# A spectral mixing and snake kernel on one Trainium2 core: batch 0's last stage in groups of 3, 5 and 4 row columns, and batch 2's input loaded behind batch 1's relayout

## The chip, the cores and the metric

The kernel runs on one core of a Trainium2 chip. The metric is the device time of one execution in microseconds (us). The core has a tensor engine for matmuls (TensorE, PE), a vector engine (VectorE, DVE), a scalar engine (ScalarE, ACT), GpSimd (POOL) and SyncE (SP); the last three and ScalarE also issue DMA transfers here. Results of matmuls go to PSUM, and are evacuated to SBUF by VectorE or ScalarE.

## The reference

Two blocks follow each other. The first filters each sequence of x (8 batches, 3008 positions, 256 channels) in the frequency domain; the second is a two-layer network on every position, with a "snake" between its layers.

```python
X = np.fft.rfft(x, axis=1)                       # x: (8, 3008, 256)
Y = X * (filt_r + 1j * filt_i)[None, :, :]
y = np.fft.irfft(Y, n=x.shape[1], axis=1)
# positions of all batches as rows: (24064, 256)
h = y @ w_in                                     # d_ff = 2048
s = np.sin(alpha * h)
out = (h + s * s / (alpha + 1e-09)) @ w_out      # (24064, 256) float32
```

## The kernel before

**The filter.** The sequence of 3008 = 32 × 94 positions is seen as 32 "row columns" (n) of 94 rows. A Fourier transform is done in two stages of small matmuls with tables, and back in two stages. For a batch from 1 on this is the class `Spectral`: `load_x` (line 140, POOL queue) brings x as 4 tiles of 8 row columns, rounded to fp16; `first` (line 180) multiplies with the table wf into PSUM tile pa, which is evacuated and stored to DRAM by the SP queue (d1, line 185); `load_t2` (line 192, POOL queue, 8 transfers a batch) reads it back in another layout: this pair is the relayout. `forward` (line 200, PSUM tile pb) has twelve steps u; ScalarE evacuates each to an fp16 tile xf (line 203), and two DMAs of the SP queue swap its halves into xs (line 207). `product` (line 214) and `cross` (lines 220 and 221) multiply with the filter on VectorE; `inverse` (line 231, PSUM tile pc) follows, stored to DRAM as d2 by the SP queue (line 238) and read back by it (`load_t4`, line 243). `last` (line 258, PSUM tile pd, 4 row columns and half the channels at a time) gives y, in fp16, with the channels on the partitions. The pools have 4 buffers for x, 3 for xf, 3 for xs, and 2 PSUM tiles for all of pa, pb, pc and pd.

**Batch 0** doesn't go through DRAM: code before the main loop does its four stages with transposes on VectorE (line 385) in place of the relayout. Its inverse stage `inverse_0` (line 422) needs the table e_t, which comes in two halves of 384 KB behind the filter's loads (line 315), all on the POOL queue. Its last stage is also in `last` (line 255: two matmuls for each row column, one for each half of the partitions). The first 8 row columns are done before the main loop (lines 488 to 492), for channels 0 to 127 and 128 to 255 in turn; the rest in the main loop, by `last_two`, a pair of groups of 4 row columns, one for each half of the channels. `evac` (lines 156 to 161) does an evacuation on ScalarE (line 159) or VectorE (line 161), by its argument or in a turn of three.

**The network** works on chunks of 512 (or 384) columns of y, that is of positions. A chunk takes 8 steps of the main loop (lines 620 to 631). In `hidden` (lines 507 to 513) two matmuls give a PSUM tile ph of 128 features, from which ScalarE makes a cosine (line 510) and VectorE the snake v (line 511). In `project` (lines 523 to 532) the chunk before is multiplied with w_out into po, copied by ScalarE (line 529) and stored by `store` (line 549), in pieces that the order of rows dictates. The pieces alternate between the SP queue and a second queue: ScalarE's for the last two tiles of the last chunk, POOL's for the other tiles of that chunk, SP again otherwise.

**The order** of all instructions is written by hand. The filter of the later batches runs between the network's matmuls: `put` (line 557) gives each of its operations a due time in steps, and `slot` (line 597) emits at every half step what is due, in that order. So the due times set what stands behind what in each engine's and each queue's order. The due times that matter here are those of x of batch 2 (line 578), of batch 0's later pairs (line 572) and, unchanged, those of batch 1's t2 loads (12.5, line 582) and of its forward steps (from 17.5, line 585).

Of the kernel before, what the change touches and what calls it, by code (L numbers as in the profile page):

```python
# [10 lines left out]
FP32 = mybir.dt.float32  # L11
# [11 lines left out]
NR = 2 * N1  # L23
NK = 4 * NS
# [38 lines left out]
def kernel(  # L63
# [10 lines left out]
    nc = tc.nc  # L74
# [6 lines left out]
    e_dram = nc.inline_tensor(e_host, name="e_tbl")  # L81
# [10 lines left out]
    def pool(name, bufs, space=None):  # L92
        kw = {} if space is None else {"space": space}
        return ctx.enter_context(tc.tile_pool(name=name, bufs=bufs, **kw))
# [11 lines left out]
    fps = pool("fps", 2, PSUM)  # L106
# [5 lines left out]
    t4_h = [cpool.tile([128, 16, C], FP16, name=f"t4_h{i}") for i in range(2)]  # L112
# [6 lines left out]
    y = cpool.tile([128, 2, 2, 32, NR], FP16)  # L119
# [4 lines left out]
    for h in range(2):  # L124
        nc.sync.dma_start(out=x32[:, 4 * C * h:4 * C * h + 4 * C],
                          in_=bass.AP(tensor=x.tensor, offset=x.offset + 4 * h * C, ap=[[32 * C, 96], [1, 4 * C]]))
    nc.scalar.dma_start(out=wf0_t, in_=wf0_dram.ap())
    d_t = cpool.tile([128, NS, 128], FP16)
    e_t = cpool.tile([128, NS, 128], FP16)
    wi_t = cpool.tile([NK, NR], FP16)  # L130
    wi0_t = cpool.tile([128, NR], FP16)
# [24 lines left out]
    def evac(dst, src, on_act=None):  # L156
        flip[0] = (flip[0] + 1) % 3
        if flip[0] if on_act is None else on_act:
            marks["act"] = nc.scalar.copy(out=dst, in_=src)  # L159
        else:  # L160
            marks["dve"] = nc.vector.tensor_copy(out=dst, in_=src)  # L161

    class Spectral:
# [79 lines left out]
            nc.sync.dma_start(out=t4_h[ch // 2][0:NK, r0:r0 + 8, :],  # L243
                               in_=self.d2_rows[:, 8 * ch:8 * ch + 8, :])

        def last(self, u, on_act=None):
            ch, rest = divmod(u, 4)
            half, cb = divmod(rest, 2)
            n0 = 8 * ch + 4 * half
            ps = fps.tile([128, 4, 128], FP32, name=f"pd_{self.b}_{u}", tag="f")  # L250
            psv = ps.rearrange("p a b -> p (a b)")[:, 0:4 * NR].rearrange("p (a r) -> p a r", r=NR)
            for i in range(4):
                if self.b == 0:
                    for k in range(2):
                        nc.tensor.matmul(out=psv[64 * k:64 * k + 64, i, :], lhsT=t4_0[cb][:, n0 + i, :, k],  # L255
                                         rhs=wi0_t, start=True, stop=True)
                else:
                    nc.tensor.matmul(out=psv[:, i, :], rhs=wi_t, start=True, stop=True,  # L258
                                     lhsT=t4_h[ch // 2][0:NK, n0 % 16 + i, cb * 128:cb * 128 + 128])
            evac(y[:, cb, self.b % 2, n0:n0 + 4, :], psv, on_act)  # L260

        def last_two(self, u):
            self.last(u, True)
            self.last(u + 1, False)

    warm = cpool.tile([128, 1], FP32)
    nc.vector.memset(warm, 0.0)
# [18 lines left out]
    def split_alpha():  # L286

        nc.gpsimd.tensor_copy(out=one[0:16], in_=id32)
        for i, part in enumerate(parts):
            src = rest if i else al  # L290
            nc.gpsimd.tensor_copy(out=part[0:16], in_=src)
            if i < 2:
                nc.gpsimd.tensor_tensor(out=rest, in0=src, in1=part[0:16], op=ALU.subtract)
# [10 lines left out]
    for g in range(2):  # L304
        gs = slice(12 * g, 12 * g + 12)
        for k, filt in enumerate((filt_r, filt_i)):
            for q in range(2):
                if (g, k, q) == (0, 1, 1):
                    split_alpha()
                off, step = ((12 * g) * C, C) if q == 0 else ((N1 - 12 * g) * C, -C)  # L310
                marks["filt", g, k] = nc.gpsimd.dma_start(
                    out=f_t[k][64 * k + 32 * q:64 * k + 32 * q + 32, gs, :],
                    in_=bass.AP(tensor=filt.tensor, offset=filt.offset + off,
                                ap=[[N1 * C, 32], [step, 12], [1, C]]))
        nc.gpsimd.dma_start(out=e_t[:, gs, :], in_=e_dram.ap()[:, gs])

    idle = opool.tile([128, 512], FP32, name="idle", tag="o")
    nc.vector.memset(idle, 0.0)
# [2 lines left out]
    def pairs(t):  # L321

        return t.rearrange("p a (b s k) -> p s (a b) k", s=32, k=2)
# [5 lines left out]
    t1_0, t2_0, g_0, t4_0 = pairs(t1_0), [pairs(t) for t in t2_0], [pairs(t) for t in t1_h], [pairs(t) for t in t4_h]  # L329
# [38 lines left out]
    for i in range(16):  # L368
        own, tag = (fps, "f") if i % 3 == 2 else (hps, "h")
        ps = own.tile([128, 512], FP32, name=f"pa_0_{i}", tag=tag)  # L370
        nc.tensor.matmul(out=ps, lhsT=wf0_t[0:NR], rhs=x0[i // 4][:, 2 * (i % 4):2 * (i % 4) + 2, :],
                         start=True, stop=True)
# [43 lines left out]
    def inverse_0(i):  # L416
# [7 lines left out]
                                 start=(k == 0), stop=(k == 1))  # L424
        evac(g_0[hc][:, 4 * w:4 * w + 4], ps.rearrange("p s (k c) -> p s c k", k=2), not (i in ()))

    w1 = cpool.tile([128, 2, DFF], FP16)
    w2 = cpool.tile([128, 16, C], FP16)
    after(nc.sync.dma_start(out=wi0_t, in_=wi0_dram.ap()), marks["filt", 0, 1])
# [2 lines left out]
    for g in range(6):  # L432
        own, tag = (t2pool, "t2") if g < 3 else (gpool, "g")
# [17 lines left out]
        if g == 0:  # L451
            after(ins, marks["products"])

    s0 = Spectral(0)

    [inverse_table(g) for g in range(2)]
    for i in range(6):
# [27 lines left out]
    for step in ([(weights_in, g) for g in range(6)] + [(s1.load_x, 0), (s1.load_x, 1)]):  # L485
        step[0](*step[1:])
    warm_pe(2)
    s0.last(0, True)
    s0.last(2, True)
    warm_pe(3)  # L490
    s0.last(1, True)
    s0.last(3, False)

    chunks = [(pb, c0, 384 if c0 == 2560 else 512) for pb in range(B // 2)
              for c0 in [*range(0, 2561, 512), *range(2944, 2 * S, 512)]]
# [19 lines left out]
    def project(k, u):  # L515

        pb, c0, n = chunks[k]
        t, half = divmod(u, 2)
        final = k == len(chunks) - 1 and t > 1
        if (t % 2 == 0 or final) and half == 0:  # L520
            pso[k] = ops.tile([128, 2, C], FP32, name=f"po_{k}_{t}", tag="o")
        for jb in range(8 * half, 8 * half + 8):
            nc.tensor.matmul(out=pso[k][:, t % 2, :], lhsT=v[k][:, jb, 128 * t:128 * t + 128],  # L523
                             rhs=w2[:, jb, :], start=(jb == 0), stop=(jb == 15))
        last = 128 * (t + 1) == n
        if half == 1 and (t % 2 == 1 or last or final):
            i0 = t % 2 if final else 0
            o = opool.tile([128, 2, C], FP32, name=f"o_{k}_{t}", tag="o")
            nc.scalar.copy(out=o[:, i0:t % 2 + 1, :], in_=pso[k][:, i0:t % 2 + 1, :])  # L529
            for i in range(i0, t % 2 + 1):  # L530
                store(o[:, i, :], pb, c0 + 128 * (t - t % 2 + i),
                      nc.scalar if final else nc.gpsimd if k == len(chunks) - 1 else nc.sync)

    def runs(cnt):

        whole = cnt if max(d for d in range(1, 17) if cnt % d == 0) > 7 else cnt - cnt % 16
        return [(0, whole), (whole, cnt - whole)] if 0 < whole < cnt else [(0, cnt)]

    def store(o_blk, pb, col, second):

        p = 0
        queues = [nc.sync, second]
        while p < 128:
            odd, rest = divmod(col + p, S)
            n2, row = divmod(rest, NR)
            cnt = min(128 - p, NR - row)
            t0 = (2 * pb + odd) * S + 32 * row + n2
            for i, (r0, rows) in enumerate(runs(cnt)):
                queues[i].dma_start(  # L549
                    out=bass.AP(tensor=out.tensor, offset=out.offset + (t0 + 32 * r0) * C,  # L550
                                ap=[[32 * C, rows], [1, C]]),
                    in_=o_blk[p + r0:p + r0 + rows, :])
            p += cnt
# [3 lines left out]
    def put(at, fn, *args, pe=False):  # L557
        pending.append((at, len(pending), pe, fn, args))
# [9 lines left out]

    for i in range(2):
        put(13 + i, negate, i)  # L570
    for u in range(4, 16, 2):
        put((1,3,4.5,6,14,16)[u // 2 - 2], s0.last_two, u, pe=True)
    for b in range(1, B):
        s = s1 if b == 1 else Spectral(b)
        z = 48 * b
        if b > 1:
            for ch in range(4):
                put((22,27,32,37)[ch] if b == 2 else z - 92 + 7 * ch, s.load_x, ch)
        for i in range(16):
            put(7.5 + 0.3 * i if b == 1 else 36 + 0.66 * i if b == 2 else z - 67 + 0.66 * i, s.first, i, pe=True)  # L580
        for g in range(4):
            put(12.5 if b == 1 else max(z - 56, 46.5), s.load_t2, g)
        for u in range(12):
            inv = 23.5 + 1.25 * u if b == 1 else 59 + 2.1 * u if b == 2 else z - 40.8 + 2.3 * u
            fwd = inv - (6 if b == 1 else 6)
            put(fwd, s.forward, u, pe=True)
            put(fwd + (0.5 if b == 1 else 1.5), s.product, u)
            if s.fused:
                put(fwd + (4 if b == 1 else 4.5), s.cross, u)
            put(inv, s.inverse, u, pe=True)  # L590
        for ch in range(4):
            put(z - (9.5 if b == 1 and ch < 3 else (10.5, 10.5, 10.5, 3)[ch]), s.load_t4, ch)
        for u in range(16):
            put(z + (u - (5 if b == 1 else 6.5) if u < 4 else 2 * u - 9), s.last, u, pe=True)
# [68 lines left out]
```

## Time and profile before

| what | before |
|---|---|
| time, median of 3 runs | 789.39 us (788.52 to 789.53) |
| span of the profiled execution | 789.0 us |
| TensorE busy | 776.2 us, 98% |
| VectorE busy | 657.4 us, 83% |
| ScalarE busy | 617.0 us, 78% |
| GpSimd busy | 79.7 us, 10% |
| bytes moved by DMA | 101.01 MB, 128 GB/s |
| granted TensorE clock | 1.00 |

In the profile, a line such as "L510 ACT" is an operation of ScalarE written at line 510. "x3" behind an operation is a count. In a timeline, the two leading numbers are the start and the duration in us, and the bracket at the end is the idle time of the engine before the operation, with what ended it. "SPq", "ACTq" and "POOLq" are the DMA issues of an engine. In the views of DMA, q0 holds what POOL issues and q1 what SP and ScalarE issue.

The early part of the run, up to about 62 us, is batch 0's filter and the weights' loads. Batch 1's filter then runs beside the network's first chunks until about 120 us, and each later batch's beside the chunks of the batches before it. The last transfers of the output end the run.

### The profile page before, as it was taken

The page shows a single profiled execution, that of the slowest core. Times are in us where ns is not written, and L with a number is a line of the kernel's source. Part 1 is how long each engine was busy: PE and PEld are TensorE (multiplying, and loading weights), DVE is VectorE, ACT ScalarE, POOL GpSimd, SP SyncE. Part 2 cuts the span into 40 slices and gives each one's busy share as a digit, 9 for nine tenths or more (in the row PEclk, how much of TensorE's full clock was granted, in tenths as well). Part 3 has the DMA queues.
Part 4 walks back from the last instruction along what each step waited for, and adds up shares of the span by engine and source line. Part 5 has one row for each costly group of instructions (what it writes and reads, how often), then busy time and mean ns, then how long its engine had stood idle before and what let it go on. Part 6 is the DMA issues. An engine that isn't in the chain of part 4 may idle for free.

```text
span 789.0 us, 16730 instructions
## 1 busy us (share of the span) xinstructions
PE 776.2 (98%) x5854; PEld 536.3 (68%) x5854; DVE 657.4 (83%) x1171; ACT 617.0 (78%) x1209; POOL 79.7 (10%) x125
## 2 busy tenths in 40 slices
PE   8999989999999999999999999999999999999997
PEld 4756757676667766777666766777666776766666
DVE  7887987899878997799978998799987999777773
ACT  6887868888878887888887888788887887777663
POOL 6442000200020000200020000200002000000000
PEclk9999999999999999999999999999999999999999
DMA  9956568755573646554575455845566233421111
GB/s 217 257 105 173 118 144 206 173 104 134 140 198 82 135 98 191 150 121 102 121 210 124 100 106 137 219 94 113 128 165 171 62 97 82 116 62 29 41 41 54
DMA packets 87677, 101.01 MB, mean 128 GB/s; under 512 B 14472, under 2 KB 75928, under 8 KB 87592
## 3 DMA queue, kind: packets, MB, share of 16 engines
q1 hardware_dynamic: 78016, 73.73, 34.5%
q0 software_dynamic: 9360, 26.15, 17.4%
q8 instruction: 46, 0.75, 0.4%
q14 instruction: 39, 0.32, 0.1%
q10 hardware_dynamic: 216, 0.05, 0.0%
HBM read 55.72 MB, written 46.66 MB: 130 GB/s over the span
## 4 chain that ended last, share of the span: by engine, by line
PE 90%; DVE 2%; DMA 2%; ACT 2%; issue 1%; POOL 1%; SPq 1%; ACTq 0%; POOLq 0%; DVEq 0%
PE po L523 40%; PE ph L507 40%; PE pa L180 3%; PE pd L258 2%; PE pb L200 2%; PE pc L231 2%; DMA e_t<-e_tbl 1%; DVE v L511 1%; PE pd L255 1%; DMA xs<-xf 1%; ACT cos_all L510 1%; DVE t_h L385 1%; SPq L549 1%; ACT t_h L159 1%; DVE t_h L161 0%
## 5 line engine op out<-in xcount | busy, mean ns | idle before, releaser
L511 DVE SCALAR_TENSOR_TENSOR v<-cos_all,ph 128x512 f16<-128x512 f32 (+1 forms) x768 | 482.8, 671 | 107.4 <-ACT cos_all L510 103.9
L510 ACT ACTIVATE cos_all<-ph 128x512 f32<-128x512 f32 (+1 forms) x768 | 410.9, 592 | 99.5 <-PE ph L507 98.3
L523 PE MATMUL po<-w,v 128*128 128x256 f16 x3008 | 388.7, 272 | 0.0
L507 PE MATMUL ph<-y,w 128*128 128x512 f16 (+1 forms) x1536 | 386.4, 374 | 0.5 <-DVE y L161 0.3
L523 PEld LDWEIGHTS <-v 128*128 128x128 f16 x3008 | 289.3, 98 | 78.2 <-issue 1.2
L507 PEld LDWEIGHTS <-w 128*128 128x128 f16 x1536 | 147.5, 98 | 104.5 <-issue 2.5
L529 ACT COPY o<-po 128x512 f32<-128x512 f32 (+1 forms) x97 | 55.6, 573 | 19.6 <-PE po L523 12.6
L203 ACT CAST xf<-pb 128x512 f16<-128x512 f32 x84 | 50.0, 595 | 15.2 <-PE pb L200 13.8
L192 POOL DMA_DIRECT2D t<-d x56 | 36.3, 666 | 202.4 <-DMA out_dram<-o 128.6
L159 ACT CAST t_h<-pa 96x512 f16<-96x512 f32 x74 | 43.3, 586 | 8.5 <-PE pa L180 8.3
L140 POOL DMA_DIRECT2D x<-in_x_dram x32 | 17.1, 535 | 302.1 <-PE pc L231 171.4
L159 ACT CAST y<-pd 128x376 f16<-128x376 f32 x83 | 40.0, 482 | 7.6 <-PE pd L258 5.3
L258 PEld LDWEIGHTS <-t_h 96*128 96x128 f16 x448 | 31.4, 97 | 18.4 <-issue 0.4
L180 PE MATMUL pa<-x,wf_t 94*96 94x512 f16 x112 | 42.2, 381 | 1.0 <-DVE t_h L161 0.6
L159 ACT CAST g<-pc 128x512 f16<-128x512 f32 x58 | 34.4, 593 | 9.4 <-PE pc L231 9.0
L221 DVE TENSOR_TENSOR p<-p,xs 128x512 f16<-128x512 f16 x84 | 35.7, 425 | 2.9
L220 DVE TENSOR_TENSOR xs<-xs,filt_t 128x512 f16<-128x512 f16 x84 | 35.0, 416 | 2.8 <-DMA xs<-xf 2.8
L258 PE MATMUL pd<-wi_t,t_h 96*128 96x94 f16 x448 | 37.1, 204 | 0.0
L214 DVE TENSOR_TENSOR p<-xf,filt_t 128x512 f16<-128x512 f16 x84 | 35.0, 416 | 0.0
L231 PE MATMUL pc<-p,e_t 128*128 128x256 f16 x168 | 32.1, 273 | 1.7 <-DVE p L221 1.7
L200 PE MATMUL pb<-t,d_t 128*128 128x256 f16 x168 | 32.1, 272 | 0.5 <-DVE g L161 0.4
L161 DVE CAST t_h<-pa 96x512 f16<-96x512 f32 x38 | 25.9, 681 | 0.7 <-PE pa L180 0.5
(66 smaller groups left out, 257.5 us busy)
## 6 DMA issues: line engine op xcount, KB each, us to landing
x<-in_x_dram POOLq DMA_DIRECT2D x30, 376.0 KB, 5.0
d<-t_h SPq DMA_DIRECT2D x28, 384.0 KB
t<-d POOLq DMA_DIRECT2D x56, 192.0 KB, 4.6
xs<-xf SPq DMA_DIRECT2D x168, 64.0 KB
d<-g SPq DMA_DIRECT2D x56, 192.0 KB
t_h<-d SPq DMA_DIRECT2D x28, 384.0 KB
out_dram<-o SPq DMA_DIRECT2D x104, 80.0 KB
w_out<-in_moe_w_out_dram SPq DMA_DIRECT2D x1, 2048.0 KB
```

The lines of the kernel that those rows point to most:

```text
L159: marks["act"] = nc.scalar.copy(out=dst, in_=src)
L180: marks["pe"] = nc.tensor.matmul(out=ps[0:NK, :], lhsT=wf_t, rhs=self.x[ch][:, 2 * j:2 * j + 2, :], start=True, stop=True)
L192: nc.gpsimd.dma_start(out=self.t2[g][64 * p:64 * p + 64, :, :], in_=self.d1[a0:a0 + 6, :, :].rearrange("s n c -> n s c"))
L200: nc.tensor.matmul(out=ps[:, i, :], lhsT=d_t[:, s, :], rhs=self.t2[s // 6][:, s % 6, :], start=True, stop=True)
L203: nc.scalar.copy(out=self.xf[u], in_=ps)
L231: nc.tensor.matmul(out=ps[:, i, :], lhsT=e_t[:, 2 * w + i, :], rhs=pt[:, i, :], start=(k == 0), stop=(k == len(pr) - 1))
L258: nc.tensor.matmul(out=psv[:, i, :], rhs=wi_t, start=True, stop=True, lhsT=t4_h[ch // 2][0:NK, n0 % 16 + i, cb * 128:cb * 128 + 128])
L507: nc.tensor.matmul(out=ps[:, 0:n], lhsT=w1[:, cb, jb * 128:jb * 128 + 128], rhs=y_cols[:, cb, c0:c0 + n], start=(cb == 0), stop=(cb == 1))
L510: nc.scalar.activation(out=cs[:, 0:n], in_=ps[:, 0:n], func=AFT.Sin, bias=float(np.pi / 2))
L511: marks["snake"] = nc.vector.scalar_tensor_tensor(out=v[k][:, jb, 0:n], in0=cs[:, 0:n], scalar=-1.0, in1=ps[:, 0:n], op0=ALU.add, op1=ALU. ...
L523: nc.tensor.matmul(out=pso[k][:, t % 2, :], lhsT=v[k][:, jb, 128 * t:128 * t + 128], rhs=w2[:, jb, :], start=(jb == 0), stop=(jb == 15))
L529: nc.scalar.copy(out=o[:, i0:t % 2 + 1, :], in_=pso[k][:, i0:t % 2 + 1, :])
```

## The change

It has four parts. The first four columns of the table e_t get a load of their own, ahead of the imaginary filter. Batch 0's last stage is cut into groups of 3, 3, 5, 5, 4, 4, 4 and 4 row columns in place of eight groups of 4: the first chunk of 512 columns needs row columns 0 to 5 only, which are now all that is done before the main loop. The two evacuations of a later pair are done by one engine, VectorE and ScalarE in turn, where each pair had one on each. The loads of x of batch 2 are due at steps 14 to 18.5 in place of 22 to 37, which puts them on the POOL queue directly behind batch 1's t2 loads, and takes them out of the time in which batch 1's later half-swaps run. And in the last chunk, the second block of a pair of tiles is stored by the POOL queue alone, which leaves SyncE's queue to the first block and to the final tiles.

```diff
@@ filter and table loads
         for k, filt in enumerate((filt_r, filt_i)):
+            if (g, k) == (0, 1):
+                nc.gpsimd.dma_start(out=e_t[:, 0:4, :], in_=e_dram.ap()[:, 0:4])
             for q in range(2):
...
-        nc.gpsimd.dma_start(out=e_t[:, gs, :], in_=e_dram.ap()[:, gs])
+        es = slice(4 if g == 0 else 12, 12 * g + 12)
+        nc.gpsimd.dma_start(out=e_t[:, es, :], in_=e_dram.ap()[:, es])
@@ batch 0's last stage
-    def last_two(self, u):
-        self.last(u, True)
-        self.last(u + 1, False)
+    def last_0(cb, n0, n1, on_act):
+        ps = fps.tile([128, 4, 128], FP32, name=f"pd_0_{cb}_{n0}", tag="f")
+        psv = ps.rearrange("p a b -> p (a b)")[:, 0:(n1 - n0) * NR].rearrange("p (a r) -> p a r", r=NR)
+        for n in range(n0, n1):
+            for k in range(2):
+                nc.tensor.matmul(out=psv[64 * k:64 * k + 64, n - n0, :], lhsT=t4_0[cb][:, n, :, k],
+                                 rhs=wi0_t, start=True, stop=True)
+        evac(y[:, cb, 0, n0:n1, :], psv, on_act)
+
+    def last_two(i, n0, n1):
+        last_0(0, n0, n1, ([i % 2 == 1] * 2)[0])
+        last_0(1, n0, n1, ([i % 2 == 1] * 2)[1])
...
-    s0.last(0, True)
-    s0.last(2, True)
+    last_0(0, 0, 3, True)
+    last_0(0, 3, 6, True)
     warm_pe(3)
-    s0.last(1, True)
-    s0.last(3, False)
+    last_0(1, 0, 3, True)
+    last_0(1, 3, 6, False)
@@ the last chunk's stores
-                      nc.scalar if final else nc.gpsimd if k == len(chunks) - 1 else nc.sync)
+                      *(nc.sync, nc.scalar) if final else (nc.gpsimd if i else nc.sync, nc.gpsimd)
+                      if k == len(chunks) - 1 else (nc.sync, nc.sync))
@@ due times
-    for u in range(4, 16, 2):
-        put((1,3,4.5,6,14,16)[u // 2 - 2], s0.last_two, u, pe=True)
+    for i, n0 in enumerate((6, 11, 16, 20, 24, 28)):
+        put((1,3,4.5,6,14,16)[i], last_two, i, n0, (11, 16, 20, 24, 28, 32)[i], pe=True)
...
-                put((22,27,32,37)[ch] if b == 2 else z - 92 + 7 * ch, s.load_x, ch)
+                put((14,15.5,17,18.5)[ch] if b == 2 else z - 92 + 7 * ch, s.load_x, ch)
```

More of the change, by code (lines that the diff above doesn't have):

```diff
@@ L244, in load_t4, with last @@
                                in_=self.d2_rows[:, 8 * ch:8 * ch + 8, :])
-        def last(self, u, on_act=None):
+        def last(self, u):
             ch, rest = divmod(u, 4)
@@ L252, in last @@
             for i in range(4):
[L253 to L260, printed above, removed]
-        def last_two(self, u):
-            self.last(u, True)
-            self.last(u + 1, False)
+                nc.tensor.matmul(out=psv[:, i, :], rhs=wi_t, start=True, stop=True,
+                                 lhsT=t4_h[ch // 2][0:NK, n0 % 16 + i, cb * 128:cb * 128 + 128])
+            evac(y[:, cb, self.b % 2, n0:n0 + 4, :], psv)
     warm = cpool.tile([128, 1], FP32)
@@ L452, in weights_in @@
             after(ins, marks["products"])
-    s0 = Spectral(0)
     [inverse_table(g) for g in range(2)]
@@ L537, in runs, with store @@
         return [(0, whole), (whole, cnt - whole)] if 0 < whole < cnt else [(0, cnt)]
-    def store(o_blk, pb, col, second):
+    def store(o_blk, pb, col, *queues):
         p = 0
-        queues = [nc.sync, second]
         while p < 128:
```

## The prediction

> **What bounds the kernel now.** I begin with the page: section 1 for the shares, section 4 for the chain that sets the end.
>
> ```profile
> PE 776.2 (98%) x5854; PEld 536.3 (68%) x5854; DVE 657.4 (83%) x1171; ACT 617.0 (78%) x1209; POOL 79.7 (10%) x125
> PE 90%; DVE 2%; DMA 2%; ACT 2%; issue 1%; POOL 1%; SPq 1%; ACTq 0%; POOLq 0%; DVEq 0%
> ```
>
> TensorE is busy for 776.2 of 789.0 us. The change keeps every matmul of the reference's work (batch 0's last stage stays at 128), so it can win only the idle 12.8 us. The second view, TensorE's waits by stretch, says where that idle time is: before 62 us, and between 62 and 140. From 140 to 780 it lists none.
>
> ```profile
> PE pd L255 <- ACT y L159: 0.6, 1, 0.6
> PE pc L422 <- DMA e_t<-e_tbl: 0.5, 1, 0.5
> ...
> PE pc L422 <- DVE p L412: 0.5, 1, 0.5
> ```
>
> These are from 0 to 62 us (total, times, longest). The third view, busy time by stretch (columns PE, PEld, DVE, ACT, POOL, clock, DMA share, GB/s), shows the one hole after that.
>
> ```profile
> 75.00:85.00 10.00, 10.00 (x73) 6.94 (x72) 8.45 (x16) 8.26 (x17) 0.00 (x0) 1.00 0.56 131
> 95.00:110.00 15.00, 14.64 (x107) 10.29 (x106) 14.83 (x32) 11.97 (x25) 1.05 (x2) 1.00 0.71 145
> 110.00:120.00 10.00, 8.11 (x53) 4.81 (x51) 7.11 (x15) 6.46 (x12) 0.00 (x0) 1.00 0.56 137
> ```
>
> In 110 to 120, TensorE lacks 1.89 us and VectorE has time too: neither engine is the limit, something is waited for. The timelines of TensorE and VectorE name it.
>
> ```profile
> 117.03 0.39 PE L231 MATMUL pc<-p,e_t 128*128 128x256 f16 x2 [1.46 <-DVE p L221]
> ```
> ```profile
> 116.09 0.42 DVE L220 TENSOR_TENSOR xs<-xs,filt_t 128x512 f16<-128x512 f16 x1 [2.83 <-DMA xs<-xf]
> ```
>
> The last half-swap (xs of u=11) of batch 1, issued at 109.57 and 110.08, is late by 2.83 us. The DMA shares by queue at 109 to 111 us (packets, MB, share of 16 engines) say why:
>
> ```profile
> q0 software_dynamic: 58, 0.23, 79.7%
> q1 hardware_dynamic: 9, 0.01, 1.5%
> ```
>
> That is the third x load of batch 2 (q0, the POOL queue, issued 107.68): while it runs, the SP queue (q1) gets almost nothing. At 98 to 100 us, behind the load issued at 96.62, it is 98.2% to 1.1%.
>
> [...] under t2 loads (71 to 77 us) q1 still has 17.1% beside q0's 81.9%; under x loads 1.1 to 1.5%. So x loads are bad neighbours for swaps wherever they stand. [...] the last POOL store took 1.86 us (782.73 to 784.59), the last SP store 1.78 (786.15 to 787.93). [...]
>
> **Part A, e_t's first 128 KB ahead of filt_i.** The first pc waits 0.54 us for e_t, at 21.53. But what follows is bound by filt_i of the second half: VectorE's copy at 25.12 waits for that DMA, the products follow, and pc of block 6 starts only at 27.05, after 0.46 us for p. Only the loop of pc and its evacuation behind it (two PSUM slots) can begin 0.4 earlier, up to the turn at 30.38, which waited 0.47 for its last evacuation. I take a gain of 0.2. The edit adds one DMA and no bytes, but puts 128 KB ahead of 12 filter rows; if all of that delay reached the turn it would cost 0.3. Range −0.2 to +0.3.
>
> **Part B, groups of 3, 5 and 4.** Before the main loop, each half takes 12 matmuls where it had 16: 4 × 0.0725 us (16 take 1.16) = 0.29, and its evacuation shrinks from 376 to 282 columns. [...] So the first ph after the wait at 36.79 comes some 0.3 earlier. The pairs of rows 6 to 11 then take 20 matmuls where 16 stood, and give the 0.29 back. The wait at 45.01 (0.56 us) is for the previous evacuation on ScalarE, by the queue's order of the two PSUM slots; with both evacuations of this pair on VectorE it goes. Against it: the next pair, 20 to 24, puts a second 478 ns on ScalarE, which has no idle time between 46.26 and 53.96. Net 0.56 − 0.48 = 0.1. The pairs at steps 14 and 16 meet idle time on either engine (0.35 to 0.5 on VectorE, 1.42 on ScalarE near 69 to 71): 0. Sum for B 0.1, from −0.3 to +1.0, the top if ScalarE catches up elsewhere. A and B: −0.3.
>
> **Part C, x of batch 2 at steps 14 to 18.5.** The loads leave 85.11, 96.62, 107.68 and 120.49, and stand behind the t2 loads on POOL (issued 69.15 to 74.37), so issue 74.4 to 76.5. The removed waits are the three of TensorE: 0.21 at 112.12, 1.46 at 117.03, 0.20 at 117.62 = 1.87. I take all of it. What the move adds: four loads of 376 KB back to back. A packet of 4 KB of such a load takes 0.324 us in the trace, and a load has 94, so 16 engines need 1.9 us for one; with the gaps between them seen before, the POOL queue holds the engines from about 77.5 to 86. In that time the SP queue issues swaps of u=0 (75.16), u=1 (78.30), stores of one chunk (79.50 to 82.77), u=2 (82.87). Who waits: a swap holds an xf buffer, and xf has three; so ScalarE's xf of u=4, at 84.10, waits for the swap of u=1, xf of u=5 (87.76) for that of u=2, and everything behind them on ScalarE (cos, evacuations) waits too, then VectorE and TensorE. If nothing of SP moved until 86, that is up to 2.4 us at 84.10 and 0.6 at 87.76; if it gets a share as beside t2, 0. ScalarE has 10 − 8.26 = 1.74 of slack in 75 to 85, and TensorE has four ph slots of work ahead of it. I take a loss of 0.3, and keep 0 and 2.4 for the range. Nothing waits for x itself sooner: its first pa comes long after.
>
> **Part D, the last chunk's stores** (the diff has it, the title not). The timelines of the end: ScalarE, SyncE's queue, POOL's.
>
> ```profile
> 784.83 0.37 ACT L529 COPY o<-po 128x256 f32<-128x256 f32 x1 [1.38 <-DMA out_dram<-o]
> ```
> ```profile
> 785.77 0.80 SPq L549 DMA_DIRECT2D out_dram<-o  x2
> ```
> ```profile
> 782.21 1.04 POOL L549 DMA_DIRECT2D out_dram<-o  x2 [182.13 <-ACT o L529]
> ```
>
> The last copy ends 785.20, but SyncE issues its two stores only at 785.77 and 786.15, since its queue is late; the last lands 787.93 and the span ends 789.0. Three issues of the tile before (0.31 + 0.32 + 0.39 and gaps = 1.17 us) go to POOL. SyncE is then free at about 784.6, and issues when the copy is there, at 785.24 (ScalarE's own store starts 785.23), and 785.62: 0.53 sooner. POOL issues five at 0.53 from 782.21, to 784.9, and with its 1.86 lands by 786.8, before SyncE's last (787.4): hidden. ScalarE's two land at 787.09, then next to the limit. Gain 0.5 (0.3 to 0.8).
>
> **The likeliest sum:** −0.3 (A, B) − 1.87 + 0.3 (C) − 0.5 (D) = −2.4: 787.0 us.
>
> **The rivals.** *The swap's wait only moves.* For it: the shares of 1.1 and 1.5% above, and VectorE's 9.64 of 10 us busy in 85 to 95, so that a stall isn't caught up. Against it: in 75 to 85 VectorE and ScalarE have 1.6 and 1.7 us free. If the move costs 1.9 in place of 0.3, C is nil; 789.4 − 0.8 = 788.6. *It becomes worse.* The swaps of u=1 and u=2 both wait for the end of the fourth load (2.4 us), and one straggling engine holds another swap as at 113 to 116 (1.9): 789.4 + 4.3 − 1.87 − 0.8 = 791.0, slower. For it: a queue that had 8 t2 loads and now 12 transfers in a row; against it: stores and swaps did get 17.1% beside the t2 loads. *The early stage wins more,* as ScalarE's queue closes up after the pair at 45 (1 us more): 786.0. For it: 1.30 us of ScalarE idle at 46.26; against it: ScalarE is then full to 53.96.
>
> **How the numbers follow.** The forecast 0.60; the wait moves 0.20; the early stage 0.12; slower 0.08. The range runs from 785.7 (below the third rival by the 0.3 at the top of D) to 789.3 (the wait that moves, with A and B at their bad ends: 788.6 + 0.7), and leaves out the slow rival and both tails. With 0.2% being 1.58 us, faster means below 787.81, slower above 790.97. Faster: 0.60 × 0.9 + 0.12 = 0.66. Same: 0.06 of the forecast's own tail and 0.18 of the first rival = 0.24. Slower: 0.08 and 0.02 from the first rival = 0.10.
>
> **What the changed profile would show.** A: no wait of pc for e_t, but the turn near 30.2 and not 29.9. B: no wait of pd for an evacuation near 45. C: no wait of over 1 us for xs in 110 to 120, TensorE at 10 of 10 there, and no x load of batch 2 after 77; wrong if ScalarE's xf near 84 and 88 wait for xs by over 1 us or TensorE falls below 9.5 in 80 to 90. D: the last store's issue at 0.05 behind the last copy; wrong if POOL's or ScalarE's stores land last. The forecast fails above all if waits that TensorE never showed before 110 appear between 77 and 95.

## The result and the profile after

The changed kernel takes 792.29 us (median; 791.88 to 793.08), the kernel before 789.43 beside it: ratio 1.004, 95% interval 1.0023 to 1.0057. A second measurement, against more runs of before, gave 792.61 and 1.0035 (1.0022 to 1.0047). So it is slower by 2.5 to 2.9 us; forecast were 2.4 us less, and a range that ended at 789.3.

The profile's span is 791.3 us, 2.3 more than before. The page's first section and chain:

```profile
PE 776.8 (98%) x5854; PEld 535.4 (68%) x5854; DVE 657.4 (83%) x1171; ACT 616.9 (78%) x1209; POOL 81.8 (10%) x129
...
PE 88%; DVE 3%; DMA 3%; ACT 2%; issue 1%; SPq 1%; POOL 0%; ACTq 0%; DVEq 0%; POOLq 0%
```

The work of each engine is what it was; only idle time was added. Where? I laid TensorE's order of both traces side by side: from batch 1's first pa on it is the same, so the difference of the two start times shows where one kernel falls behind. It is +0.19 us at the first ph (36.27 against 36.08), −0.15 at batch 1's first pa (49.77 against 49.92) and +0.22 at its fourth (53.42 against 53.19; the expectations below call this one the first). From 85.9 to 102.9 it grows to +3.47. At 117 to 119 it falls to +1.41, and stays there to the last matmul. From the start of the last matmul to the end of the span, before needs 4.50 us and after 5.36. So 0.22 + 3.25 − 2.06 + 0.86 = 2.27.

Busy time by stretch (columns as before): first the stretch of before that the prediction gave in words only, then after.

```profile
85.00:95.00 10.00, 10.00 (x75) 7.06 (x73) 9.64 (x21) 8.84 (x18) 0.55 (x1) 1.00 0.57 120
```
```profile
75.00:85.00 10.00, 10.00 (x71) 6.86 (x70) 6.75 (x13) 6.49 (x13) 1.77 (x4) 1.00 1.05 226
85.00:95.00 10.00, 9.03 (x60) 5.59 (x59) 8.26 (x18) 8.43 (x18) 0.00 (x0) 1.00 0.49 122
95.00:110.00 15.00, 14.12 (x99) 9.31 (x98) 14.83 (x32) 12.54 (x25) 0.00 (x0) 1.00 0.51 118
110.00:120.00 10.00, 9.67 (x65) 6.14 (x64) 9.90 (x21) 7.13 (x14) 0.00 (x0) 1.00 0.47 117
```

The hole at 110 to 120 is nearly closed (9.67 where 8.11 stood). But VectorE, 8.45 and 9.64 in the first two stretches before, now has 6.75 and 8.26: 3.08 us less work done, at a DMA share of 1.05 where 0.56 stood. In 95 to 110 VectorE is as full as before, 14.83 of 15, so it doesn't catch up there, and TensorE falls back. ScalarE's and VectorE's timelines show what they waited for:

```profile
84.54 0.59 ACT L203 CAST xf<-pb 128x512 f16<-128x512 f32 x1 [2.59 <-DMA out_dram<-o]
...
87.57 0.59 ACT L203 CAST xf<-pb 128x512 f16<-128x512 f32 x1 [1.45 <-DMA out_dram<-o]
```
```profile
84.56 0.42 DVE L220 TENSOR_TENSOR xs<-xs,filt_t 128x512 f16<-128x512 f16 x1 [1.78 <-DMA out_dram<-o]
```

These are the casts of u=3 and u=4, and the cross of u=0. The profile names an output store, because its semaphore moved at the same moment, 84.55. An xf buffer isn't freed by a store: xf of u=3 needs the buffer of u=0, and its two half-swaps (issued 75.40 and 75.96) land at 82.90 and 84.44. Those of u=1 land at 85.93 and 87.47, just before the cast of u=4. (A transfer's semaphore rises in 16 steps in the trace; the last one is taken as its landing.) Before, the two halves of u=0 landed at 80.18 and 80.34, those of u=1 at 80.52 and 80.83. The POOL queue's issues, and the shares of the queues at 76 to 80 us, after and (second fence) before:

```profile
74.60 1.14 POOL L140 DMA_DIRECT2D x<-in_x_dram  x2
75.93 0.52 POOL L140 DMA_DIRECT2D x<-in_x_dram  x1 [0.19 <-issue]
77.72 0.52 POOL L140 DMA_DIRECT2D x<-in_x_dram  x1 [1.27 <-PE pb L200]
```
```profile
q0 software_dynamic: 258, 0.82, 101.8%
q8 instruction: 1, 0.02, 2.1%
q1 hardware_dynamic: 14, 0.01, 1.2%
```
```profile
q0 software_dynamic: 126, 0.35, 42.8%
q1 hardware_dynamic: 241, 0.20, 23.9%
```

From 76.5 to 79.5 the SP queue moved one packet of 4 bytes. From 80 to 86 it moved 321 packets beside 304 of the x loads, about one for one; but 265 of its packets were of 1 KB and the others of 4 bytes, and 257 of those of x of 4 KB, and its packets took 0.05 us on the mean where those of x took 0.27, so it had 16.7% of the engines and x 86.9%.

SyncE's own queue stood still as well. In both traces, at 75 to 92 us, each of its transfers waits for the one eight issues earlier, with which it shares a semaphore. After the change its issues at 82.92, 84.46, 85.94 and 87.53 follow within 0.06 us the four landings above. So seven stores that took 3.27 us before took 5.92, and the swap of u=2, whose xf was cast from 79.93, left at 87.53 in place of 82.87. After and (second fence) before:

```profile
80.35 5.92 SPq L557 DMA_DIRECT2D out_dram<-o  x7
87.53 4.48 SPq L207 DMA_DIRECT2D xs<-xf  x6
```
```profile
79.50 3.27 SPq L549 DMA_DIRECT2D out_dram<-o  x7
82.87 1.11 SPq L207 DMA_DIRECT2D xs<-xf  x2
```

The tail, POOL's queue and ScalarE's last copy after:

```profile
783.62 2.64 POOL L557 DMA_DIRECT2D out_dram<-o  x5 [182.12 <-ACT o L537]
```
```profile
786.25 0.37 ACT L537 COPY o<-po 128x256 f32<-128x256 f32 x1 [1.38 <-DMA out_dram<-o]
```

SyncE issues its last two stores at 786.64 and 787.01, so the first comes 0.40 behind the start of the last copy, where before it came 0.94 behind: as forecast. Its closing drain starts at 789.35. But GpSimd's closing drain ends at 790.51, 4.24 behind the end of its last store's issue (786.27). Before it ended at 787.25, 4.00 behind the same point (783.25) and ahead of SyncE's at 788.25.

### The profile page after: what moved, and what is told of

Its sections match the earlier page's. It is cut to its first block, busy times and chain, and to the rows that moved or that the text cites. A ratio compares the mean times of both kernels' runs of the same rounds, so it can differ in the third digit from the quotient of the medians.

```text
span 791.3 us, 16732 instructions
## 1 busy us (share of the span) xinstructions
PE 776.8 (98%) x5854; PEld 535.4 (68%) x5854; DVE 657.4 (83%) x1171; ACT 616.9 (78%) x1209; POOL 81.8 (10%) x129
## 4 chain that ended last, share of the span: by engine, by line
PE 88%; DVE 3%; DMA 3%; ACT 2%; issue 1%; SPq 1%; POOL 0%; ACTq 0%; DVEq 0%; POOLq 0%
PE po L531 39%; PE ph L515 39%; PE pa L180 3%; PE pd L253 2%; PE pc L231 2%; PE pb L200 2%; DVE v L519 1%; DMA xs<-xf 1%; PE pd L427 1%; DMA x<-in_x_dram 1%; DMA filt_t<-in_filt_i_dram 1%; ACT cos_all L518 1%; ACT t_h L159 1%; DVE t_h L379 1%; SPq L557 1%
## 5 line engine op out<-in xcount | busy, mean ns | idle before, releaser
L159 ACT CAST y<-pd 128x376 f16<-128x376 f32 (+2 forms) x83 | 39.6, 480 | 7.8 <-PE pd L253 5.3
```

## The experiments

Each ran beside runs of before; ratios are against those. All times are medians. First each part alone.

**Part A alone** (e_t's first 128 KB ahead of filt_i).

> Kernel before with part A alone (e_t's first 128 KB loaded ahead of filt_i). Theory 1: the extra load holds back the filter's loads, so the copy of filt_i's second half, at 25.12 us before and 25.81 after the whole change, comes about 0.6 us late here too, the first turn starts at about 30.9 in place of 30.4, and the time is 0.3 to 0.6 us over before, 789.9. Rival: the copy is late for another reason than this load (a scatter of the start); then the copy is at 25.1, the first pc 0.15 to 0.5 us sooner, and the time is 0.2 us under before.

```diff
+            if (g, k) == (0, 1):
+                nc.gpsimd.dma_start(out=e_t[:, 0:4, :], in_=e_dram.ap()[:, 0:4])
...
+        es = slice(4 if g == 0 else 12, 12 * g + 12)
```

789.45 us against 789.96, 0.9995 (0.9984 to 1.0006). The copy stood at 25.39, the turn at 30.43: neither theory can be told from no effect.

**Part B alone** (groups of 3, 5 and 4).

> Kernel before with part B alone (groups of 3, 5 and 4 row columns, both evacuations of a pair on one engine). Theory 1: the groups give back a little of what the table's load costs (TensorE's first main-loop matmul was 0.19 us late after the change, while the turn was 0.48 late), so alone they make the first ph about 0.3 us sooner and leave 0.1 to 0.3 us at 60 us: time 789.2. Rival: the second evacuation on ScalarE at the pair of rows 20 to 24 costs more than the wait at 45 us that goes; then batch 1's first pa (53.19 before) is later and the time 789.7.

```diff
...
-        put((1,3,4.5,6,14,16)[u // 2 - 2], s0.last_two, u, pe=True)
+        put((1,3,4.5,6,14,16)[i], last_two, i, n0, (11, 16, 20, 24, 28, 32)[i], pe=True)
```

788.81 us, 0.9981 (0.9971 to 0.9992): 1.2 us under before by the medians, 1.5 by the ratio, better than either theory. The first ph came 0.86 sooner, batch 1's fourth pa 0.90; but 0.57 of it was there at the first matmul of batch 0's last stage (32.17 against 32.74), which part B doesn't touch. In this profile VectorE waited only 0.1 us for the swap of u=11, which gave TensorE another 2.05 us by 119; 0.7 of them were lost again at 129.

**Part C alone** (x of batch 2 behind the t2 loads).

> Kernel before with part C alone (x of batch 2 due at steps 14 to 18.5). Theory 1: the four loads take the DMA engines from SyncE's swaps, the swaps of u=0 and u=1 land at about 84.5 and 86.5 in place of 80.3 and 80.8, ScalarE waits about 4 us in all for its xf buffers, TensorE falls back 3.2 us between 85 and 103, and gets 2.1 back at 110 to 118: 1.1 us over before, 790.5. Rival: the fall at 85 needs the shifted early stage of parts A and B; then C alone has waits under 1 us there, and the time is 1.5 us under before, 787.9.

```diff
-                put((22,27,32,37)[ch] if b == 2 else z - 92 + 7 * ch, s.load_x, ch)
+                put((14,15.5,17,18.5)[ch] if b == 2 else z - 92 + 7 * ch, s.load_x, ch)
```

791.35 us, 1.0013 (1.0005 to 1.0021). TensorE's distance from before went from −0.33 to +2.77 between 85 and 103, a loss of 3.10, and 2.05 came back at 117 to 119. The rival is out: C needs no other part to fail.

**Part D alone** (three stores to POOL).

> Kernel before with part D alone (three of the last chunk's stores moved from SyncE to POOL). Theory 1: GpSimd's closing drain ends 4.0 to 4.3 us after the issue of its last store (787.25 after 783.25 before, 790.51 after 786.27 with the whole change) and now ends last, so the span ends 0.9 us later: 790.3. Rival: the tail of the changed kernel was late because of a single slow store; then SyncE's last store is issued 0.5 us sooner and the time is 788.9.

```diff
...
-                      nc.scalar if final else nc.gpsimd if k == len(chunks) - 1 else nc.sync)
+                      *(nc.sync, nc.scalar) if final else (nc.gpsimd if i else nc.sync, nc.gpsimd)
+                      if k == len(chunks) - 1 else (nc.sync, nc.sync))
```

790.36 us, 1.0006 (0.9994 to 1.0018), unclear by time. By the profile Theory 1: from the start of the last matmul the tail took 5.34 us, as after the whole change, with five issues on POOL from 782.32 to 784.94 and GpSimd's drain last, 4.24 us behind.

**The whole again, and the starvation in doses.**

> The changed kernel once more, beside the same runs of before as the next three. If the four parts add up, it takes what they took alone against before (0.9995, 0.9981, 1.0013 and 1.0006 multiply to 0.9995): 0.4 us under before. If the 2.9 us of its first measurement are its own, the parts act on each other: 1.0025 or more.

792.61 us, 1.0035. The parts alone don't add up to it: in time each is known to about 1 us only (the traces come closer, below), since the runs of before themselves spread from 788.1 to 792.7. So later I undid parts in the changed kernel, whose runs stay within 791.8 to 793.4.

> Kernel before with only two of batch 2's four x loads moved behind the t2 loads (due 14 and 15.5) and the other two due at 34 and 37. Theory 1 (x loads hold the engines, in proportion to their bytes): they end at about 82 in place of 86, the swaps of u=0 land at about 81 to 82, before xf of u=3 needs the buffer; ScalarE's waits of 4.0 us for them fall under 0.5, TensorE loses under 0.3 at 85 to 103, and the wait of 2.8 us at 116 is gone too: 1.5 to 2 us under before. Rival (any x load among the swaps costs the same, since a queue is shut out whole): the waits stay at over 2 us and the time is like that of all four, 1 us over before.

```diff
-                put((22,27,32,37)[ch] if b == 2 else z - 92 + 7 * ch, s.load_x, ch)
+                put((14,15.5,34,37)[ch] if b == 2 else z - 92 + 7 * ch, s.load_x, ch)
```

790.94 us, 1.0011 (1.0002 to 1.0019). The time is the rival's, the trace stands between the two. TensorE's loss at 85 to 103 was 2.05 where four loads cost 3.10: the wait of ScalarE for u=1 went, but the one for u=0 stayed whole, 2.9 us, and VectorE's 2.1 with it. The SP queue moved nothing here from 77.0 to 78.5, and 15 of the 16 steps of u=0's second half were there only at 83.28, the last at 83.85. By then the x loads were all but done: three of their packets ran at 83 to 84 us. So half of the loads did the whole harm to the first swap. A new wait came too: 1.0 us of TensorE for t4 of batch 1 at 129, beside the loads due at 34 and 37.

> Kernel before with only the third x load of batch 2 later (due 34 in place of 32), behind the last swaps of batch 1. Theory 1 (that load alone starves the swap of u=11): VectorE's wait of 2.83 at 116 and TensorE's 1.46 at 117 are gone, 1.3 to 1.9 us under before, and a smaller scatter from run to run, since the swap's race with the load goes. Rival (the swap is late because of out stores and d2 stores on the SP queue itself): the wait stays and the time is as before.

```diff
-                put((22,27,32,37)[ch] if b == 2 else z - 92 + 7 * ch, s.load_x, ch)
+                put((22,27,34,37)[ch] if b == 2 else z - 92 + 7 * ch, s.load_x, ch)
```

789.30 us, 0.9987 (0.9978 to 0.9996), 0.8 to 1.0 us under before and short of Theory 1's 1.3. The wait of cross for u=11 is gone. So it is in the three other profiles with this load at 34 and in all with part C, while seven of the eight with it at 32 or 33 have 0.7 to 3.0 us: the third load was what made the swap late. But 0.7 us for t4 at 129 are new, and in this profile the second load made a swap late too, at 102 (1.9 us of ScalarE).

> Part C alone, with 5 buffers for xf in place of 3 (and 3 for g in place of 4, to make room). Theory 1 (the late swaps act through the xf buffers that they hold, and through VectorE's product that needs them): ScalarE's waits of 2.6 and 1.5 for xf go; VectorE's 1.8 at cross of u=0 stays; TensorE's loss at 85 to 103 falls from 3.1 to 1 to 1.5 us: 0.5 to 1 us under before. Rival (the late half-swaps stop VectorE alone, ScalarE's wait is beside it): the loss stays about 3 us, and the time 1 us over before, as with 3 buffers.

```diff
-    xfpool = pool("xf", 3)
+    xfpool = pool("xf", 5)
...
-    gpool = pool("gp", 4)
+    gpool = pool("gp", 3)
...
-                put((22,27,32,37)[ch] if b == 2 else z - 92 + 7 * ch, s.load_x, ch)
+                put((14,15.5,17,18.5)[ch] if b == 2 else z - 92 + 7 * ch, s.load_x, ch)
```

790.01 us, 1.0004 (0.9997 to 1.0011): 0.7 us less, by the ratios, than C with three buffers. ScalarE's waits went; this line of VectorE stayed:

```profile
84.14 0.42 DVE L220 TENSOR_TENSOR xs<-xs,filt_t 128x512 f16<-128x512 f16 x1 [1.89 <-DMA xs<-xf]
```

TensorE's loss was 1.93 where it was 3.10. So in this pair of profiles somewhat over a third of the loss goes through the xf buffers, and the rest stays without them. VectorE's own wait for the swap is the one wait for it that is left, and SyncE's queue still stood (the swap of u=2 left at 86.58). Theory 1 had the split right and the rest too small. That g has a buffer less here was not tried alone.

**The parts undone in the changed kernel**, and x ahead of the t2 loads.

> The changed kernel without part A (e_t in its two old loads). Theory 1: A holds back filt_i: the copy of its second half stood at 24.7 to 25.1 us in five of the six kernels without A, and at 25.4 to 26.1 in the three with it; so without A the copy is back at about 25.0, the first turn at 30.0, and the time 0.7 us under the changed kernel's 792.6: 791.9. Rival: scatter of the start only; the time stays at 792.6, or is higher by the e_t wait of 0.5.

```diff
-            if (g, k) == (0, 1):
-                nc.gpsimd.dma_start(out=e_t[:, 0:4, :], in_=e_dram.ap()[:, 0:4])
...
-        es = slice(4 if g == 0 else 12, 12 * g + 12)
```

792.53 us, 1.0042 (1.0028 to 1.0057), beside the whole's 1.0040 and 1.0035: no change. The copy stood at 25.47 without A; the start scatters that much. So the rival holds: part A is worth nothing that shows. The next two ran on the same chip, and are read against this one.

> The changed kernel without part B (groups of 4 as before; parts A, C and D stay). Theory 1: B alone put the first ph 0.86 us and batch 1's first pa 0.90 us earlier in one profile, some of it scatter of the start; so without it the time is 0.3 to 0.8 us over the changed kernel's 792.6: 793.1. Rival: beside A, B gains nothing or costs (an evacuation more on ScalarE); then 792.0 to 792.6.

```diff
...
-        put((1,3,4.5,6,14,16)[i], last_two, i, n0, (11, 16, 20, 24, 28, 32)[i], pe=True)
+        put((1,3,4.5,6,14,16)[u // 2 - 2], s0.last_two, u, pe=True)
```

792.89 us, 1.0047 (1.0032 to 1.0062), 0.4 over the kernel without A: B seems to gain a little, as Theory 1 had it, but 0.4 alone is within what the start scatters. The traces are sharper. From the first matmul of batch 0's last stage to batch 1's fourth pa, the ten profiles with part B need 20.11 to 20.20 us and the ten without it 20.34 to 20.51: 0.27 on the mean.

> The changed kernel without part D (the last chunk's stores as before; parts A, B and C stay). Theory 1: GpSimd's closing drain no longer ends last, the end comes 4.5 us after the start of the last matmul in place of 5.4: 0.9 us under the changed kernel's 792.6, 791.7. Rival: drains and stores of the end lie beside each other; 792.6 or, as D was meant, 0.5 more.

```diff
...
-                      *(nc.sync, nc.scalar) if final else (nc.gpsimd if i else nc.sync, nc.gpsimd)
-                      if k == len(chunks) - 1 else (nc.sync, nc.sync))
+                      nc.scalar if final else nc.gpsimd if k == len(chunks) - 1 else nc.sync)
```

791.75 us, 1.0033 (1.0018 to 1.0048), 0.8 under the kernel without A; the tail took 4.6 us where it took 5.4. So D costs 0.8.

> Kernel before with three of batch 2's x loads ahead of batch 1's t2 loads (due 9, 10, 11), as soon as batch 1's x buffers come free, and the fourth behind batch 1's second stage (due 40). Theory 1: between 55 and 66 us no swap is on its way and the DMA engines are busy for 0.34 to 0.55, so the loads cost nothing there, and all of what they cost among the swaps is gone, the late swap at 116 with it: 1.5 to 2.3 us under before. Rival: they hold back batch 1's d1 stores and with them the t2 loads (69.15) and pb; then a new wait of TensorE of 1 to 3 us stands at 70 to 76, and the time is that of before or more.

```diff
-                put((22,27,32,37)[ch] if b == 2 else z - 92 + 7 * ch, s.load_x, ch)
+                put((9,10,11,40)[ch] if b == 2 else z - 92 + 7 * ch, s.load_x, ch)
```

792.01 us, 1.0043 (1.0027 to 1.0058): the rival. TensorE's waits at 62 to 140 us:

```profile
PE pb L200 <- DMA t<-d: 2.8, 1, 2.8
PE pa L180 <- DMA x<-in_x_dram: 0.9, 1, 0.9
PE pb L200 <- DVE g L161: 0.4, 1, 0.4
```

The t2 loads were issued from 72.47 in place of 69.15; the 0.9 is at 133.20, for the load due at 40. With these due times x ahead of the relayout costs as well.

**What C is worth, and a version that beats both.**

> The changed kernel without part C (x of batch 2 due at 22, 27, 32, 37 as before; parts A, B and D stay). Theory 1 (C costs 3.1 at 85 to 103 and gives back the late swap at 116, which took 2 us in the profile of before, but 0 to 2 from run to run): 1 to 2.5 us under the changed kernel's 792.6, so 790.1 to 791.6, with the wider scatter of before. Rival (the other parts cost most of it): within 0.5 us of 792.6.

```diff
-                put((14,15.5,17,18.5)[ch] if b == 2 else z - 92 + 7 * ch, s.load_x, ch)
+                put((22,27,32,37)[ch] if b == 2 else z - 92 + 7 * ch, s.load_x, ch)
```

789.76 us, 1.0012 (1.0003 to 1.0020), 2.85 under the whole by the medians of two chips, 1.8 by the ratios: Theory 1. In this profile the swap of u=11 made VectorE wait 0.72 us, and TensorE had no wait over 0.4 us from 62 on.

> Kernel before with the three stores of the last chunk on ScalarE's queue in place of POOL's. Theory 1 (in part D, POOL's closing drain was what came last): POOL issues two stores as before and its drain ends before SyncE's last store lands; SyncE issues its last two stores at the last copy's end, 0.5 us sooner, and the time is 0.3 to 0.5 us under before. Rival (fewer stores on SyncE gain nothing, the last store's landing is set elsewhere): as before, or 0.3 over, if the issues hold ScalarE's copies up.

```diff
...
-                      nc.scalar if final else nc.gpsimd if k == len(chunks) - 1 else nc.sync)
+                      *(nc.sync, nc.scalar) if final else (nc.scalar if i else nc.sync, nc.gpsimd)
+                      if k == len(chunks) - 1 else (nc.sync, nc.sync))
```

789.33 us, 1.0000 (0.9988 to 1.0011): no gain in time that can be told. In the profile the tail took 4.09 us in place of 4.50, and SyncE's last two stores were issued from 785.00, 0.53 behind the start of the last copy. The two later kernels with these stores have tails of 4.00 and 3.97; the eleven with the old stores have 3.98 to 5.04. So the shorter SyncE queue does no harm; POOL's longer one did.

> Part B, batch 2's x loads spaced (due 22, 27, 34, 40), 5 buffers for xf and 3 for g, and the last chunk's three stores on ScalarE's queue. Theory 1: early stage 0.3 to 0.7 sooner, no wait for a swap of over 0.5 us between 75 and 120 (1 us less on average), tail 0.3 to 0.5 sooner: 1.8 to 2.5 us under before. Rival: what is gained in one place is lost to the next DMA wait (t4 of batch 1 at 129); then no more than 1 us under before.

> As the last one with the tail of before. Theory 1: 1.5 to 2 us under before, and 0.3 to 0.5 us over the kernel with the stores on ScalarE's queue. Rival: as there, no more than 0.7 us under before.

Part B in both, the stores on ScalarE's queue in the first, and (against the changed kernel):

```diff
-    xfpool = pool("xf", 3)
+    xfpool = pool("xf", 5)
...
-    gpool = pool("gp", 4)
+    gpool = pool("gp", 3)
...
-                put((14,15.5,17,18.5)[ch] if b == 2 else z - 92 + 7 * ch, s.load_x, ch)
+                put((22,27,34,40)[ch] if b == 2 else z - 92 + 7 * ch, s.load_x, ch)
...
```

789.88 us, 1.0011 (1.0004 to 1.0019), and 790.02, 1.0012 (0.9997 to 1.0026): the rival. No swap made an engine wait over 0.2 us, but in the first TensorE waited 2.1 us for t4 at 129, in the second not at all. The load at 34 runs beside the stores and loads of batch 1's second relayout; which of them is late differs between these two profiles. Whether the one buffer less for g has a part in it was not tried.

> Part B and the third x load due at 33 in place of 32. Theory 1: the load leaves behind the swap of u=11 and ends before batch 1's second relayout (d2 and t4), so neither waits: 1.5 to 2 us under before, like or a little better than part B alone (0.9981). Rival: the place of one load among so many transfers gains one wait for another; then 0 to 1 us under before, worse than part B alone.

> The same with the last chunk's three stores on ScalarE's queue. Theory 1: 0.3 us under the same without it. Rival: no difference, as the stores on ScalarE's queue alone made none that could be told (1.0000, 0.9988 to 1.0011).

```diff
...
-                put((14,15.5,17,18.5)[ch] if b == 2 else z - 92 + 7 * ch, s.load_x, ch)
+                put((22,27,33,37)[ch] if b == 2 else z - 92 + 7 * ch, s.load_x, ch)
```

With part B, 788.81 us, 0.9986 (0.9974 to 0.9998): about 1 us under before, the size that the rival gave. With the stores on ScalarE's queue as well, 788.32 us, 0.9982 (0.9975 to 0.9988). The last one is below before in time, and further below the changed kernel, with the smallest scatter of those with 14 runs or more (787.7 to 789.1). But Theory 1's reason doesn't hold: the load didn't leave behind the swap of u=11, but 0.9 and 0.7 us ahead of it, and VectorE still waited for that swap 1.38 and 1.19 us, of which TensorE lost 0.6 and 0.4. Its stretches show neither hole; the 0.38 us at 95 to 110 are nearly before's:

```profile
85.00:95.00 10.00, 10.00 (x75) 7.06 (x73) 9.86 (x22) 8.84 (x18) 0.12 (x1) 1.00 0.53 116
95.00:110.00 15.00, 14.62 (x108) 10.26 (x106) 14.83 (x31) 11.96 (x25) 1.06 (x2) 1.00 0.69 147
110.00:120.00 10.00, 9.66 (x62) 5.80 (x60) 8.74 (x17) 7.72 (x15) 0.52 (x1) 1.00 0.69 159
```

By ratio it can't be told from part B alone (0.9981).

## Why the prediction was wrong

**Part C, the loss taken as 0.3.** This is the step that failed, and the largest: it cost TensorE 2.7 to 3.3 us, 3.0 on the mean of the six profiles that have part C and three xf buffers. The prediction had the POOL queue's hold of the engines to about 86, and it ended near there (56 KB of x in the half microsecond from 86 on, 16 in that from 87). It named the swap of u=0 among those on the way, but priced only the waits for u=1 and u=2, on xf of u=4 and u=5. The waits came a step sooner: xf of u=3 for u=0 (2.59), xf of u=4 for u=1 (1.45). Even so, "up to 2.4 us at 84.10 and 0.6 at 87.76" was written down, and was near in size. What was wrong is the choice of 0.3, argued from ScalarE's 1.74 us of slack and the ph slots. The slack that counts is VectorE's: it waits itself for cross of u=0, does 3.08 us less work by 95, and is full for the 15 us that follow. Its 14.83 of 15 stood in a line the prediction showed. Nor did the prediction ask what late landings do to SyncE's queue, where each transfer waited for the one eight issues earlier: four issues from 82.92 to 87.53 came within 0.06 us behind four late landings. The share of 17.1% that SyncE had beside t2 loads was no argument: the x loads came behind t2 loads, and left it 1.2% at 76 to 80.

**Part C, the gain taken as 1.87.** The place was right, and the third load was the cause. In the trace of before the wait cost TensorE 2.05 us. But its length comes from one late piece. In that trace VectorE was ready for the swap of u=11 at 113.26; 15 of the 16 steps of its second half were there by 113.53, and the last at 116.00, 0.86 us behind the last step of the x load. The six profiles with the old due times:

| kernel | last step of the third x load, behind its 15th | VectorE's wait for the swap | cost to TensorE |
|---|---|---|---|
| before | 2.67 us | 2.83 us | 2.05 us |
| part A alone | 0.95 | 1.36 | 0.6 |
| part B alone | 0.08 | 0.10 | 0 |
| part D alone | 2.71 | 3.02 | 2.2 |
| changed, without C | 0.72 | 0.72 | 0 |
| stores on ScalarE's queue | 1.91 | 2.06 | 1.3 |

The 15th step of the load comes 4.5 to 4.8 us behind its issue in all six; the last one is 0.1 to 2.7 us later still, and VectorE waits about as long. How far behind the load the swap is issued (1.9 to 2.7 us) doesn't order the waits. Why one piece is late, and not always, is open. So one profile overstated what the typical run could give: 1.0 us on the mean of the six. By that C costs 3.0 − 1.0 = 2.0. In time it cost 1.0 to 1.4 alone, and 1.8 to 2.9 beside the other parts.

**Part D, −0.5.** SyncE's stores did come 0.54 sooner behind the last copy, and POOL's did land ahead of SyncE's last. The step "lands by 786.8: hidden" failed: what counts of a store on POOL here isn't its landing but the end of GpSimd's closing drain, 4.24 us after the end of the last issue (786.27 to 790.51; before 783.25 to 787.25). With that as the price, the prediction's own 784.9 for the fifth issue gives 789.1, behind the end of SyncE's work. Measured: +0.8 in time; in the traces 5.34 to 5.36 us of tail in the six profiles with D, and 4.43 on the mean of the eleven with the old stores: +0.9. (The landing of the last POOL store of before is 784.65 in the trace, 1.92 us behind its issue and not 1.86.)

**Parts A and B, −0.3.** A: 0.2 forecast, none seen. The wait for e_t goes, but it isn't in the profile of the changed kernel without A either. The first matmul of batch 0's last stage stands at 32.15 to 33.47 in the six profiles with A and at 32.17 to 33.39 in the fourteen without. B: 0.1 forecast, 0.27 in the traces. It gains 0.3 ahead of the first ph, as forecast, and 0.4 from there to batch 1's first pa. (An evacuation of 376 columns took 482 ns on ScalarE and 542 on VectorE on the mean of before, one of 282 columns 395 and 451 after: 0.09 us less on either engine.) Between the first and the fourth pa it loses 0.37 (3.65 us against 3.28, in every profile with and without it), where pa waits for an evacuation on ScalarE. That fits the second evacuation of the pair of rows 20 to 24, which the prediction had put at 0.48. Why B is 1.2 to 1.5 us in time alone is open: two profiles with it and the old due times of x have short waits for u=11 (0.1 and 0.72, where four without it have 1.36 to 3.02), but they are too few.

**The sum by the traces:** 0 (A) − 0.3 (B) + 2.0 (C) + 0.9 (D) = 2.6, for 2.5 to 2.9 measured. It is an estimate from the profiles named above; in time the parts alone don't give it, since each is known to about 1 us only.

**The rivals.** "It becomes worse" gave 791.0 and had 0.08. It is the nearest, and in part by luck: it priced the swaps of u=1 and u=2 in place of u=0 and u=1, added a second late swap of 1.9 that the profiles with C don't show, and left −0.5 for D in the sum. The fuller line of VectorE should have given it more weight. The range was also summed too narrow: A and B at their own bad ends are 0.9 above what was taken, not 0.7, which makes its upper end 789.5. The measured time lies beyond that too.

**What no run here shows** is why the SP queue moved one packet from 76.5 to 79.5 us, beside 189 of the POOL queue, and from 80 to 86 about as many packets as that queue, 321 to 304.

## What to carry to other kernels

A large load is not free because its data is needed late: ask which small transfers that an engine waits for are on the way in those microseconds (here half-swaps of 64 KB beside loads of 376 KB: waits of 2.59 us on ScalarE and 1.78 on VectorE), and price the wait at the engine that has no slack behind it (here VectorE, busy for 14.83 of the next 15 us), not only at the one that waits first. Ask also whether late landings stop the queue that issues the next transfers (here seven stores took 5.92 us where they took 3.27). A wait that hung on the last of 16 pieces was 2.83 us in one profile here and 0.10 in another: take several profiles before its whole length is booked as a gain. And count a queue's tail up to the drain that closes it (on POOL here 790.51), not to the last landing (787.66).

## What was not expected of the hardware

- Beside x loads in 4 KB packets, SyncE's queue of 1 KB packets got 16.7% of the engines at 80 to 86 us, with 321 packets to 304.
- Of the 16 steps of the third x load, 15 were there 4.5 to 4.8 us behind its issue in six profiles, and the last 4.6 to 7.5 us. A swap beside it ended 0.9 to 1.2 us behind that last step.
- GpSimd's closing drain ended 4.24 us after the end of its last store's issue in all six profiles with five stores on that queue, and 4.0 in all fourteen with two. Beside that the landing of the last store varied from 1.2 to 1.7 us behind the end of its issue. SyncE's last store needed 1.8 to 1.9 from issue to landing.
